# Row maxima in unequal column steps, and one VectorE instruction moved behind a transposition, in a routed-attention and feed-forward kernel

## The chip, the cores and the metric

The kernel runs on one core of one Trainium2 chip. The metric is the device time of one execution in microseconds (us); lower is better. A core has five engines that run at once, each through its own instructions in order: TensorE (PE in the profile; its weight loads are listed apart as PEld), VectorE (DVE), ScalarE (ACT), GpSimd (POOL) and SyncE (SP), which here only issues transfers. They wait for each other through semaphores. TensorE writes to PSUM, 128 partitions by 8 banks of 512 float32 values; everything else lives in SBUF.

## The reference

Two parts follow each other. The first is an attention in which a query sees only the keys that chose the same one of 16 centroids; the second is a feed-forward block on its output.

```python
batch, n_heads, seq, head_dim = (4, 8, 768, 64)      # n_clusters = 16
q_assign = np.argmax(np.einsum('bhsd,hcd->bhsc', q_n, c_n), axis=-1)
k_assign = np.argmax(np.einsum('bhsd,hcd->bhsc', k_n, c_n), axis=-1)
mask = q_assign[:, :, :, None] == k_assign[:, :, None, :]
scores = scale * np.matmul(q, k.transpose(0, 1, 3, 2))
scores = np.where(mask, scores, -1000000000.0)
scores = scores - np.max(scores, axis=-1, keepdims=True)
attn = np.exp(scores)
attn = attn / (np.sum(attn, axis=-1, keepdims=True) + 1e-09)
return np.matmul(attn, v).astype(np.float32)
...
h = x @ w_in                                          # x: 3072 x 512, w_in: 512 x 2048
sp = np.maximum(h, 0.0) + np.log1p(np.exp(-np.abs(h)))
g = h * erf(sp)
return (g @ w_out).astype(np.float32)
```

## The kernel before

The attention goes over 16 blocks `p`, each a batch and two heads; the two heads sit in partitions 0 to 63 and 64 to 127 and are worked on side by side. A block has 12 units: two halves of 384 queries, times six groups of 128 keys. A unit is a score matrix of 128 keys by 384 queries for both heads in a two-bank PSUM tile `sc`, of which there are two in turn. `products` (line 512) starts it with float32 products of keys and queries, `scores` (527) adds in bfloat16 the mask and the negative row maximum of each query (through `km` and `qm`), `curve` (541) takes the exponential on ScalarE into one of the eight tiles `pr`, `accumulate` (550) sums these on GpSimd, `attend` (562) multiplies them by the values on TensorE into `turned[half]`, and `divide` (575) normalizes a finished half.

The maximum of a query's row must be known before its scores. `maxima_step` (463) finds it half a block ahead: for a group `t` of 128 queries (`t` = 0 to 5) and one part of the keys, a bfloat16 pass over `qv` and `kv` and a pass over the masks `qm` and `km` fill the two-bank tile `wide`, one bank for each head, and a VectorE reduction over the part's columns writes the negative maximum into `nmx`. Each group of queries takes two such steps, over 384 keys each. There is one tile `wide`: a step can't start before the reduction of the step in front of it has read it. After three groups a small reduction writes `lowest`, and `turn` (494) transposes it into a row of `qm`.

`period(p, i)` (1345), six for each block, writes out the order of the work: two units and one group of queries, `t` = (i + 3) mod 6. On TensorE: the transposed `lowest` (i = 0, 3), the first maxima step, the products of two units, the first pass of the second step, the scores of the first unit, the second pass of the second step (on the array rows that the scores leave free), the scores of the second unit, `pick` matmuls that spread masks (`masks`, 437, in i = 0, 2, 5), the `similarities` (394) of block p + 2 with the centroids in i = 3, and the 32 matmuls of `attend` for the two units before. In i = 0 and 3 `divide` follows: its four sums go into `turned[1 - half]`, in i = 3 `turned[1]`, where the similarities of the same period lie until VectorE has transposed them.

`choose` (407) takes these similarities on VectorE: a transposition into `sims`, a maximum over each 16 (`mx`), a comparison (`hot`), and transpositions of that. In i = 3 `mx` is put into spare columns of the second unit's tile, `sc_of[u + 1]`, so this tile is free for its next unit, the second of i = 4, only when `hot` has read it.

Beside this, the weights of the second part are decoded from their transferred words, in pieces of 128 x 512 (28 of 32 pieces during the attention): `size`, `rest` and `sign` on ScalarE, `bounded` (322, a maximum with 2) and `shifted` (330, a shift left, on the result of `bounded`) on VectorE, `summed` (334) on GpSimd. A block decodes two pieces, one of which has `bounded` and `shifted` in i = 0, the other in i = 3, between the instructions of `choose`.

After the attention comes the feed-forward part, in a form with seven products of quarter matrices in place of eight; neither the diff nor the prediction goes into it.

All helpers record their instructions through one wrapper, so that nearly every row of the profile carries line 138; rows are told apart by the names of their tiles.

Of the kernel before, what the change touches and what calls it, by code (L numbers as in the profile page):

```python
# [14 lines left out]
ALU = mybir.AluOpType  # L15
ACT = mybir.ActivationFunctionType
AX = mybir.AxisListType
PSUM = bass.MemoryType.PSUM

P = 128  # L20
B, H, S, D = 4, 8, 768, 64
# [4 lines left out]
HW = S // 2  # L26
QW = HW // 2
TW = QW + 1
HJ = NJ // 2
HP = H // 2  # L30
NPAIR = B * HP
DM, DFF = H * D, 2048
NFT = DFF // P
# [113 lines left out]
def kernel(  # L147
# [53 lines left out]
    nbig = const.tile([P, 1], F32, name="nbig")  # L201
    ccT = const.tile([P, HP, 2 * C], F32, name="ccT")

# [22 lines left out]
    def heads(p):  # L226
        return p // HP, 2 * (p % HP)

    def load(p, nm, src, pl):
        if p >= NPAIR:  # L230
            return
        b, h0 = heads(p)
        if nm == "v":
            t = pl.tile([P, NJ, 2, D], F32, name="in_v")
            for e in range(2):
                queues[0].dma_start(out=t[:, :, e], in_=src[b, h0 + e].rearrange("(j p) d -> p j d", p=P))
        else:

            if pl is None:
                t = x_more.rearrange("p a k t -> p (a k t)")[:, (nm == "k") * S : (1 + (nm == "k")) * S]  # L240
                t = t.rearrange("p (n t) -> p n t", t=Q)
            else:
                t = pl.tile([P, NB, Q], F32, name="in_" + nm)
            for e in range(2):
                for g in range(D // Q):
                    queues[e if nm == "q" else e * g].dma_start(
                        out=t[e * D + g * Q : e * D + (g + 1) * Q],
                        in_=src[b, h0 + e, :, g * Q : (g + 1) * Q].rearrange("(n t) d -> t n d", t=Q),
                    )
        pairs.setdefault(p, {})[nm] = t  # L250
# [22 lines left out]
    for base, pattern, sign, op, fill in (  # L273
# [5 lines left out]
            out=first, in_=first, compare_op=op, fill=fill, base=base, pattern=pattern,  # L279
# [38 lines left out]
    def size_and_rest(n):  # L318
        size(n)
        rest(n)  # L320

    def bounded(n):
        w = w_steps[n][0]
        ve.tensor_scalar(out=w, in0=w, scalar1=2.0, scalar2=None, op0=ALU.max)
# [5 lines left out]
    def shifted(n):  # L330
        w = w_steps[n][0].bitcast(U32)
        ve.tensor_scalar(out=w, in0=w, scalar1=3, scalar2=None, op0=ALU.logical_shift_left)
# [8 lines left out]
    for e in range(2):  # L341
        for n in range(2):
            r = e * D + n * Q
# [37 lines left out]
    def transposes(p, which="qk"):  # L381

        if p >= NPAIR:
            return
# [9 lines left out]
    def similarities(p):  # L394

        if p >= NPAIR:
            return
        st = pairs[p]
        st["psim"] = turned[1][:, 0:HW]
        for g in range(4):  # L400
            te.matmul(
                st["psim"][2 * C * g : 2 * C * (g + 1)], lhsT=ccT[:, p % HP],
                rhs=st["qk"[g // 2] + "T"][:, (g % 2) * HW : (g % 2 + 1) * HW],
# [3 lines left out]
    def choose(p, spare=None, aside=False):  # L407

        if p >= NPAIR:
            return  # L410
# [22 lines left out]
    def vectors(p, nm):  # L433
        if p < NPAIR:
            ae.copy(out=pairs[p][nm + "v"], in_=pairs[p][nm + "T"])

    def masks(p, nm, half, bank, narrow=False, copied_by=ae):

        if p >= NPAIR:
            return lambda: None  # L440
# [22 lines left out]
    def maxima_step(p, i, sm=wide, behind=False):  # L463

        st = pairs[p]
        nmx = maxima[p % 2]
        t, half = divmod(i, 2)

        def passes(a, b, start, rows):
            for e in range(2):  # L470
                r = slice(e * D + rows.start, e * D + rows.stop)
                te.matmul(
                    sm[:, e, 0:HW], lhsT=st[a][r, t * P : (t + 1) * P],
                    rhs=st[b][r, half * HW : (half + 1) * HW], start=start, stop=not start,
                )

        passes("qv", "kv", True, slice(0, D))
        if behind:
            yield
        passes("qm", "km", False, slice(Q, D) if behind else slice(0, D))  # L480
        if behind:
            yield
        ve.tensor_reduce(
            out=nmx[:, :, t, half], in_=sm[:, :, 0:HW], axis=AX.X, op=ALU.max, negate=True
        )
        if i in (NJ - 1, 2 * NJ - 1):
            h = i // NJ
            ve.tensor_reduce(
                out=lowest[h][:, :, ::D].rearrange("p t e -> p e t"),
                in_=nmx[:, :, h * HJ : (h + 1) * HJ], axis=AX.X, op=ALU.min,  # L490
            )
            turns.append((p, h))
# [82 lines left out]
    def divide(u):  # L575
# [30 lines left out]
        )  # L606
        b, r = divmod(p, HP)
        for g in range(4):
# [717 lines left out]
    def run(work):  # L1326
        for _ in work:
            pass
# [16 lines left out]
    def period(p, i):  # L1345
        u = 2 * NJ * p + 2 * i
        n1, n2 = 2 * p - 1, 2 * p
        early = lambda n: 0 <= n < N_EARLY

        def mask(place):  # L1350
            which = (MASKS if p else FIRST_MASKS).get((i, place))
            if which:
                return masks(p + 1, *which, turned[0 if i in (0, 5) else 1], place > 1, ve if i == 0 else ae)
            return lambda: None

        if u > 0:
            for which in turns if i in (0, 3) else ():
                turn(*which)
                turns.remove(which)
            step_ahead(u)  # L1360
        mask(0)()
        next(part[0], None)
        if i == 5:
            next(routing[0], None)
        if i == 0 and p:
            run(routing[0])
        if u == 2:
            next(routing[0])
        products(u)
        products(u + 1)  # L1370
        mask(1)()
        second = step_ahead(u + 1, True) if u > 0 else iter(())
        next(second, None)
        rows = D if u == 0 or u + NJ >= len(units) else Q
        scores(u, rows)
        next(second, None)
        if i:
            next(second, None)
        next(part[0], None)
        scores(u + 1, rows)  # L1380
        later = mask(2)
        if i == 0:
            later()
            later = lambda: None
            next(second, None)
        if i == 3:
            similarities(p + 2)
            routing[0] = choose(p + 2, sc_of[u + 1][:, 0], True)
        curve(u)
        later()  # L1390
        curve(u + 1)
        if u == 0:
            step_ahead(1)
            similarities(1)
            routing[0] = choose(1, turned[0])
            next(routing[0])
            next(routing[0])
            vectors(1, "q")
            vectors(1, "k")
        if i == 0 and early(n1 - 1):  # L1400
            bounded(n1 - 1)
            shifted(n1 - 1)
            sign(n1 - 1)
        elif i == 1 and early(n1):
            size_and_rest(n1)
        elif i == 3 and early(n1):
            bounded(n1)
            sign(n1)
        elif i == 5 and early(n2):
            rest(n2)  # L1410
        for _ in range(min(len(forms), FORMS.get(p, {}).get(i, 0))):
            forms.pop(0)[0]()
        if i == 3:
            next(routing[0], None)
            if early(n1):
                shifted(n1)
            for _ in range(2):
                next(routing[0], None)
        elif i == 1:
            load(p + 1, "v", v, vp)  # L1420
            if p == 0:
                run(routing[0])
                transposes(2, "q")
        elif i == 2:
            transposes(p + 2, "k")
        elif i == 4:
            vectors(p + 2, "k")
            vectors(p + 2, "q")
        elif i == 5:
            transposes(p + 3, "q")  # L1430
        if u > 0:
            if i in POOL_FORMS.get(p, ()) and forms:
                forms.pop(0)[1]()
            if i == 1 and early(n1 - 1):
                summed(n1 - 1)
            elif i == 4 and early(n1):
                summed(n1)
            for w in (u - 2, u - 1):
                accumulate(w)
            for w in (u - 2, u - 1):  # L1440
                attend(w)
            if i % HJ == 0:
                part[0] = divide(u - 1)
                next(part[0])
        if i == 3 and early(n2):
            size(n2)
# [11 lines left out]
    st = pairs[0]  # L1458
    st["qT"], st["kT"] = rows[0]["q"], rows[0]["k"]
    ve.transpose(out=st["qT"], in_=st.pop("q").rearrange("p n t -> p (n t)"))  # L1460
    for e in range(2):
        ve.tensor_copy(
            out=ccT[e * D : (e + 1) * D, :, e * C : (e + 1) * C],
            in_=pct[e * D : (e + 1) * D].rearrange("d (r e c) -> d r e c", e=2, c=C)[:, :, e],
# [7 lines left out]
    for r in (0, D):  # L1472
        for half in range(2):
            for e in range(2):
                c = r + half * Q + e * C
                ve.tensor_copy(
                    out=pick[r : r + D, half, e * D : (e + 1) * D].rearrange("p (n c) -> p n c", n=2)[:, :, 1 : C + 1],
                    in_=first[r : r + D, c : c + C].unsqueeze(1).to_broadcast([D, 2, C]),
# [174 lines left out]
```

## Time and profile before

| | |
|---|---|
| time, median of 3 runs | 960.74 us (960.52 to 960.83) |
| the profiled execution: time, span | 960.8 us, 959.1 us |
| granted TensorE clock in it | 1.00 of full speed |
| the 192 maxima reductions on VectorE, 128 x 768 values each | 0.955 us each, 183 us in all |
| their matmuls, two passes, 2 x 378 | 63.9 and 62.6 us busy |
| attention, about 30 to 410 us: TensorE, VectorE, ScalarE, GpSimd busy | 380.0, 321.8, 288.0, 314.0 us |
| the rest, 410 to 959 us: the same | 545.3, 451.1, 238.7, 216.0 us |

The span is the time from the first to the last instruction in the trace; the device time is a little longer. In a timeline a row has the start, the time it took, the engine, the operation with the tile written and the tile read, the shape, and how many instructions were merged. An instruction is named by its tiles: `nmx<-wide` is a maxima reduction, `wide<-kv,qv` and `wide<-km,qm` are the two passes of a step, `sc<-...` with float32 (from `qT,kT`, or from `more_out`, where every third block keeps its `qT` and `kT`) are products, `sc<-qm,km` scores, `turned<-pr,in_v` is `attend`, `turned<-more_out,minus` the sums of `divide`. A VectorE `TENSOR_SCALAR` on `w_in` or `w_out` is `bounded` with type f32 and `shifted` with type uint32. Matmul rows overlap: their durations hold the passage through the array, so the distance of two starts tells what a matmul costs, not its duration.

### The profile page before, as it was taken

The numbers are of one execution on the slowest core, as the hardware profiler recorded it, in microseconds if no ns is written. First come the engines' busy times: TensorE is split into PE (matmuls) and PEld (weight loads), VectorE is DVE, ScalarE is ACT, GpSimd is POOL, SyncE is SP. The second block draws the span as 40 slices with busy tenths as digits, with TensorE's granted clock in tenths as the row PEclk, the third lists the DMA queues.
The fourth block names the chain that finished last, engine by engine and source line by source line (L and its number), as shares of the span: only waits on it lengthen the run. The fifth ranks groups of instructions, "written<-read, shape, count | busy, mean of one in ns | idle before, by whom it ended". The sixth has DMA issues, their size and how long they took to land.

```text
span 959.1 us, 22447 instructions
## 1 busy us (share of the span) xinstructions
PE 951.2 (99%) x8954; PEld 727.5 (76%) x8954; DVE 797.8 (83%) x1395; ACT 538.7 (56%) x815; POOL 538.3 (56%) x375
## 2 busy tenths in 40 slices
PE   8999999999999999999999999999999999999998
PEld 3555555555555555588888888998999899989987
DVE  8888888888888887787689889688868987897887
ACT  3777777777777777542524431654257236525541
POOL 1688888878888888897579910360054016203600
PEclk9999999999999999999999999999999999999999
DMA  9355444444454522041403444463444436343533
GB/s 217 68 112 112 111 111 111 112 112 111 90 119 83 133 54 57 21 151 55 177 1 154 157 161 145 130 199 110 154 133 165 116 126 210 110 149 121 159 112 110
DMA packets 172313, 116.06 MB, mean 121 GB/s; under 512 B 131376, under 2 KB 141104, under 8 KB 172208
## 3 DMA queue, kind: packets, MB, share of 16 engines
q1 hardware_dynamic: 169280, 113.41, 42.5%
q8 instruction: 71, 1.16, 0.5%
q10 hardware_dynamic: 2928, 1.21, 0.4%
q14 instruction: 34, 0.28, 0.1%
HBM read 90.21 MB, written 24.38 MB: 119 GB/s over the span
## 4 chain that ended last, share of the span: by engine, by line
PE 96%; DVE 2%; ACT 1%; issue 0%; DMA 0%; DVEq 0%; SPq 0%; ACTq 0%
PE bank L138 42%; PE turned L138 32%; PE sc L138 17%; PE wide L138 6%; DVE nmx L138 1%; ACT a_s L138 0%; ACT L138 0%; DVE g L138 0%; DMA in_q<-in_q_dram 0%; DVE kT L138 0%; DVE osb L138 0%; DVE g_more L138 0%; DVE sims L138 0%; DVE qT L138 0%; DVE turned L138 0%
## 5 line engine op out<-in xcount | busy, mean ns | idle before, releaser
L138 POOL TENSOR_TENSOR more_out<-more_out,pr 128x768 f32<-128x768 f32 x128 | 217.1, 1696 | 16.2 <-ACT pr L138 6.8
L138 DVE TENSOR_REDUCE nmx<-wide 128x2 f32<-128x768 f32 x189 | 180.5, 955 | 46.4 <-PE wide L138 45.9
L138 ACT ACTIVATE pr<-sc 128x768 f32<-128x768 f32 x192 | 148.7, 810 | 87.4 <-PE wide L138 68.7
L138 POOL TENSOR_TENSOR g<-g 128x512 f32<-128x512 f32 x36 | 47.1, 1310 | 217.2 <-DVE g L138 215.3
L138 PE MATMUL turned<-pr,in_v 128*32 128x193 f32 x3072 | 144.8, 330 | 0.0
L138 PEld LDWEIGHTS turned<-pr,in_v 128*32 128x32 f32 x3072 | 91.5, 109 | 50.7 <-issue 21.3
L138 PE MATMUL sc<-qT,kT 64*128 64x384 f32 x528 | 98.4, 486 | 0.0
L138 DVE TENSOR_TENSOR g<-g 128x512 f32<-128x512 f32 x114 | 79.0, 693 | 16.5 <-PE bank L138 12.9
L138 DVE TENSOR_TENSOR g<-a_s,g 128x512 f32<-128x512 f32 x80 | 73.4, 944 | 5.6 <-ACT a_s L138 5.6
L138 DVE TENSOR_TENSOR g<-bank,g 128x256 f32<-128x256 f32 (+1 forms) x129 | 63.8, 522 | 15.3 <-PE bank L138 8.1
L138 PE MATMUL bank<-w_out,g 128*128 128x256 f32 x328 | 75.7, 380 | 0.0
L138 ACT ACTIVATE a_s<-g 128x1024 f32<-128x1024 f32 (+1 forms) x36 | 41.0, 1149 | 56.1 <-POOL g L138 45.5
L138 PE MATMUL bank<-g_more,g 128*128 128x256 f32 x304 | 71.8, 379 | 0.0
L138 PE MATMUL bank<-x_own,w_in 128*128 128x128 f32 (+1 forms) x432 | 71.6, 308 | 0.0
L138 POOL TENSOR_TENSOR more_out<-pr,pr 128x768 f32<-128x768 f32 x32 | 58.9, 1840 | 20.3 <-ACT pr L138 20.3
L138 PEld LDWEIGHTS bank<-w_out,g 128*128 128x128 f32 x328 | 62.0, 190 | 9.6 <-issue 1.4
L138 PEld LDWEIGHTS <-qv 64*128 64x128 bf16 x384 | 27.0, 93 | 53.4 <-issue 37.4
L138 PEld LDWEIGHTS sc<-qT,kT 64*128 64x128 f32 x528 | 49.2, 187 | 22.0 <-ACT inv L138 3.1
L138 ACT ACT_TABLE_LOAD x40 | 51.3, 1283 | 24.3 <-DVE g L138 23.7
L138 PE MATMUL wide<-kv,qv 64*128 64x384 bf16 x378 | 63.9, 328 | 1.1 <-ACT km L138 0.6
L138 PEld LDWEIGHTS bank<-x_own,w_in 128*128 128x128 f32 x432 | 61.1, 191 | 4.0 <-issue 0.6
L138 PEld LDWEIGHTS bank<-g_more,g 128*128 128x128 f32 x304 | 57.8, 190 | 7.8
(242 smaller groups left out, 2065.5 us busy)
## 6 DMA issues: line engine op xcount, KB each, us to landing
g_more<-b_dram SPq DMA_DIRECT2D x48, 512.0 KB, 3.6
g_more<-w_dram SPq DMA_DIRECT2D x84, 256.0 KB, 2.8
x_own<-in_moe_w_in_dram SPq DMA_DIRECT2D x13, 512.0 KB, 5.1
in_v<-in_v_dram SPq DMA_DIRECT2D x32, 192.0 KB, 3.2
x_dram<-more_out SPq DMA_DIRECT2D x128, 48.0 KB, 1.7
x_own<-x_dram SPq DMA_DIRECT2D x6, 1024.0 KB, 5.5
in_k<-in_k_dram SPq DMA_DIRECT2D x59, 96.0 KB, 2.7
in_q<-in_q_dram SPq DMA_DIRECT2D x58, 96.0 KB, 4.9
```

Source lines behind the costliest of these rows:

```text
L138: ins = getattr(self.engine, name)(*args, **kw)
```

## The change

The columns of the two maxima steps of a group of queries become unequal: 256 and 512 keys for `t` = 0, 1, 3, 4, and 352 and 416 for `t` = 2 and 5. Both steps keep their place, their number of instructions and their sum of 768 keys. In period i = 3 `bounded` moves behind the next step of `choose`, which is the transposition into `sims`, and so comes directly in front of `shifted`; `sign`, on ScalarE, stays. On the other engines' queues and for the transfers the order is as it was.

```diff
+KEYS = (S - 512, S - 512, 352)
...
         t, half = divmod(i, 2)
 
+        n = KEYS[t % HJ]
+        keys = (slice(0, n), slice(n, S))[half]
+        n = keys.stop - keys.start
+
         def passes(a, b, start, rows):
             for e in range(2):
                 r = slice(e * D + rows.start, e * D + rows.stop)
                 te.matmul(
-                    sm[:, e, 0:HW], lhsT=st[a][r, t * P : (t + 1) * P],
-                    rhs=st[b][r, half * HW : (half + 1) * HW], start=start, stop=not start,
+                    sm[:, e, 0:n], lhsT=st[a][r, t * P : (t + 1) * P],
+                    rhs=st[b][r, keys], start=start, stop=not start,
                 )
...
         ve.tensor_reduce(
-            out=nmx[:, :, t, half], in_=sm[:, :, 0:HW], axis=AX.X, op=ALU.max, negate=True
+            out=nmx[:, :, t, half], in_=sm[:, :, 0:n], axis=AX.X, op=ALU.max, negate=True
         )
...
         elif i == 3 and early(n1):
-            bounded(n1)
             sign(n1)
...
         if i == 3:
             next(routing[0], None)
             if early(n1):
+                bounded(n1)
                 shifted(n1)
             for _ in range(2):
                 next(routing[0], None)
```

(S is 768, HW 384, HJ 3, P 128, D 64.)

## The prediction

> **What bounds the kernel now.** I read the page's shares first, then its chain of waits, then the timeline of one block of heads (head pair 11) engine by engine, and last the waits of the weight loads.
>
> ```profile
> PE 951.2 (99%) x8954; PEld 727.5 (76%) x8954; DVE 797.8 (83%) x1395; ACT 538.7 (56%) x815; POOL 538.3 (56%) x375
> ...
> PE 96%; DVE 2%; ACT 1%; issue 0%; DMA 0%; DVEq 0%; SPq 0%; ACTq 0%
> ```
>
> TensorE sets the end: 96% of the chain. Taken alone, this says that only streamed columns count and that VectorE, 83% busy, has room. The timeline says where it has none. First TensorE, period i=3 (starts and durations in us; below I use the trace's starts to the nanosecond):
>
> ```profile
> 299.80 0.34 PE L138 MATMUL wide<-kv,qv 64*128 64x384 bf16 x2
> 299.97 0.33 PE L138 MATMUL wide<-km,qm 64*128 64x384 bf16 x2
> 300.13 1.45 PE L138 MATMUL sc<-more_out 64*128 64x384 f32 x8
> 301.42 0.33 PE L138 MATMUL wide<-kv,qv 64*128 64x384 bf16 x2
> 301.68 0.33 PE L138 MATMUL sc<-qm,km 32*128 32x384 bf16 x2
> 301.69 0.34 PE L138 MATMUL wide<-km,qm 32*128 32x384 bf16 x2
> 301.85 0.32 PE L138 MATMUL sc<-qm,km 32*128 32x384 bf16 x2
> 302.11 0.52 PE L138 MATMUL turned<-qT,ccT 128*32 128x384 f32 x2
> ```
>
> The first maxima step of a period is the pair at 299.80 and 299.97, the second the pairs at 301.42 and 301.69. The two heads of a pair start 3 ns apart and run side by side, so a pass over 384 columns costs 0.16 to 0.17. The second pass of the second step (301.69) runs beside the scores of the first unit (301.68), and the scores of the second unit follow at 301.85. From one first step to the next there are 3.757 us in a period where TensorE waits for nothing (i=1 or 4 of the last blocks).
>
> Now VectorE from the second reduction of i=3 on, and the weight load that waits for it:
>
> ```profile
> 302.13 0.96 DVE L138 TENSOR_REDUCE nmx<-wide 128x2 f32<-128x768 f32 x1 [0.83 <-PE wide L138]
> ...
> 303.00 0.42 DVE L138 TENSOR_SCALAR w_out<-w_out 128x512 f32<-128x512 f32 x1
> 303.33 0.58 DVE L138 STREAM_TRANSPOSE sims<-turned 128x384 f32<-128x384 f32 x1
> 303.83 0.39 DVE L138 TENSOR_SCALAR w_out<-w_out 128x512 uint32<-128x512 uint32 x1
> 304.14 0.55 DVE L138 TENSOR_REDUCE sc<-sims 128x24 f32<-128x384 f32 x1
> 304.72 0.55 DVE L138 TENSOR_TENSOR hot<-sims,sc 128x384 bf16<-128x384 f32 x1
> 305.20 0.95 DVE L138 TENSOR_REDUCE nmx<-wide 128x2 f32<-128x768 f32 x1
> ```
>
> ```profile
> 305.39 0.33 PEld L138 LDWEIGHTS sc<-more_out 64*128 64x128 f32 x4 [0.34 <-ACT inv L138]
> ```
>
> VectorE runs without a gap from 302.13 to the reduction at 305.20. `hot` reads `mx`, which lies in the spare columns of the second unit's `sc` tile, so the next product into that tile waits for it. `hot` ends at 305.278; TensorE's queue passes a wait on VectorE's semaphore 0.040 later, the weight load starts 0.116 after `hot`, the product 0.226 after. In all 13 blocks (head pairs 1 to 13) these distances repeat within 3 ns. The profile names ACT as releaser, but ACT's `inv` had ended at 305.079. So this chain already meets TensorE to within 30 ns.
>
> The third place is i=0, where the second reduction stands behind the copy `km`:
>
> ```profile
> 314.80 0.62 DVE L138 TENSOR_SCALAR km<-turned,nbig 128x384 bf16<-128x384 f32 x1 [0.55 <-PE turned L138]
> 315.33 0.95 DVE L138 TENSOR_REDUCE nmx<-wide 128x2 f32<-128x768 f32 x1
> ...
> 316.20 0.92 DVE L138 TENSOR_SCALAR w_out<-w_out 128x512 f32<-128x512 f32 x2
> ...
> 316.36 0.34 PE L138 MATMUL wide<-kv,qv 64*128 64x384 bf16 x2
> ```
>
> That reduction ends at 316.283, and the first step of i=1 overwrites `wide` at 316.358: 0.075 apart, of which 0.054 is the handover (read where a pass does wait, i=4: 306.149 to 306.203). The slack is 0.02.
>
> **The change, columns first.** In i=0, 1, 3, 4 the first step has 256 columns and the second 512; in i=2, 5 they have 352 and 416. The 128-column matmuls of `lowest` start 0.055 apart, so 128 columns are worth 0.054. A first step saves two passes: 0.107 (0.027 in i=2, 5). In the second step the first pass costs 0.053 more (0.013). Its second pass costs nothing: started at 0.007 after the scores, it streams 0.22, while the scores of the second unit hold TensorE until 0.33. Where a `pick` matmul follows (i=0, 2, 5) it uses the same array rows as one half of that pass and waits for it, which gives back the gain: 0 in these. So TensorE gains 0.053 in each of i=1, 3, 4, if nobody makes it wait. The float32 weights behind the narrower pass were usable 0.09 to 0.11 after their load began (296.04, 305.39), the pass now lasts 0.107: I take 0, at worst 0.02 in each of 62 periods, 1 us in all.
>
> **Reductions.** 384 values take 0.550 (the row above at 304.14), 768 take 0.955: 1.055 ns a value. The short one becomes 0.69, the long one 1.225 (+0.265); in i=2, 5 they move by 0.067.
>
> **i=3 and i=4, times from the start of i=3 (299.798).** TensorE comes to the second step's second pass 0.053 earlier (0.107 won, 0.053 lost) and streams it 0.053 longer, so the reduction behind it still starts at 2.328; it ends at 3.553. Independent VectorE instructions start about 0.085 before the one in front ends, dependent ones 0.035 after. `sims` 3.468 to 4.044; the bound, now behind it, 3.968 to 4.386; the shift, which reads what the bound wrote and now stands right behind it, 4.421 (not 4.30) to 4.807; `mx` 4.724 to 5.277; `hot` 5.312 to 5.866. Before, `hot` ended at 5.480: 0.386 later, of which 0.265 is the reduction and 0.121 the move. What the move protects is real: the sums of `divide` (304.08, 4.286) need `turned[1]` free; with `sims` ending at 4.044 and 0.12 to 0.15 of handover they keep their new time 4.233. With the bound ahead they would be about 0.3 late.
>
> The product into the second unit could start at 5.547 but starts at 5.866 + 0.226 = 6.09. It runs 0.645 and 0.03 for its later half, so the second step comes at 6.77 at the latest; the short reduction (5.784 to 6.474) is not late. Scores at 7.08 (0.258 + 0.053 later), `attend` 0.427, the next first step 1.447 after that: i=5 starts at 8.954, before at 8.550. Plus 0.404 a block. Queued behind on VectorE are `den`, two products on `turned` and the second reduction of i=4; it ends at about 8.77, just in time.
>
> A rule of the Trainium skill speaks here, "VectorE: DVE Perf Modes", section "The DRAIN you can't avoid": chained operations cost the same with or without a semaphore between them, so the move by itself would be free. The trace disagrees: bound and shift back to back in i=0 start 0.490 apart (316.199, 316.689), while in i=3 the bound is followed after 0.332.
>
> **i=0.** `pick` ends as before (2.384 against 2.388 after the start of i=0), so `km` and the long reduction start as before; it ends 0.265 later, and i=1 starts at 4.33 instead of 4.089: plus 0.24. If the cover of 0.02 were larger, by so much less.
>
> **i=1.** Its short reduction ends at 1.38 after the start, the products at 1.519: TensorE no longer waits here. The mean of 14 such periods, 3.803, becomes 3.706: minus 0.10.
>
> **Others.** i=2 and i=5: 0, at worst 0.03 each if `lowest` (0.07 to 0.08 later) makes its transposition wait, 1 us in all. Blocks 0, 14 and 15, without bound or without similarities, together minus 0.15. The six reductions at the start, in the chain one after another, keep their sum and start 0.1 earlier. What follows the attention is bound by TensorE from the first matmul (it idles under 0.1 us between 396 and 950), so the delay reaches the end. ACT, POOL and the DMA queues keep their instructions and order.
>
> Sum: 13 x (0.404 + 0.24 - 0.10) = 7.1, less 0.2 is 6.9. The profiled execution took 960.8 (span 959.1 and 1.7 around it), 0.06 above the median: **967.7 us**, slower by 0.7%.
>
> **Rivals.**
> A, the move costs nothing: the shift follows the bound as closely as an independent instruction does, `hot` ends 0.121 earlier, 13 x 0.12 = 1.6 less: 966.1. For it: no instruction was added. Against: the pair in i=0. (It is what the skill's rule above says.)
> B, the named releaser is right and the product waits for ACT. Then the second step of i=4 waits for the short reduction alone, 6.474 + 0.054 = 6.53 instead of 6.77: 13 x 0.23 = 3.0 less: 964.7. For it: the label in brackets. Against: 40 ns behind `hot`, 13 times.
> C, faster: TensorE's columns decide alone, as the 96% suggest, and VectorE's lateness is covered everywhere. 16 blocks x 3 periods x 0.053, 13 waits of 0.05 in i=4 and 14 of 0.045 in i=1: 3.9 less, 956.9. It decides only if `hot` ends by 5.547 - 0.226 = 5.32 and the long reduction of i=0 by 4.03; worked out are 5.87 and 4.28.
> D, the second unit's scores wait until the 512-column pass has ended: 0.053 in four periods and 0.013 in two, 0.24 a block over 15.5 blocks: 3.7 more, 971.4. For it: matmuls start in order here. Against: those scores start at 301.85 on array rows of their own.
>
> **How the numbers follow.** Forecast 0.62, A 0.10, B 0.12, C 0.07, D 0.09. The range leaves out C and D: from B's 964.7 less 0.7 for the slopes, to the forecast plus the two worst cases of 1 us and 0.8 for the handovers, 964.0 to 970.5. About 0.2% is what a measurement here can tell from no change: faster 0.07 (C), within it 0.05 (B with a smaller stall in i=0), slower 0.88.
>
> **What would show it.** Right: reductions of 0.69 and 1.22; bound and shift 0.45 or more apart in i=3; `hot` 0.39 later from the start of i=3; a gap of half a microsecond in front of the second unit's product in i=4; i=0 at 4.33; i=5 at 8.95 after i=3. Wrong: reductions that do not scale, a product that starts while `hot` runs, or periods i=4 and i=0 near 3.7 and 4.09.

## The result, and the profile after

The changed kernel takes 970.23 us (median of 5 runs, 970.13 to 970.32), the kernel before 960.83 in the same comparison (960.52 to 961.2): a ratio of 1.0097, 95% interval 1.0086 to 1.0108. It is slower by 9.4 us, where 6.9 were forecast; the time lies inside the range. The profiled execution has a span of 968.5 us, before 959.1.

The page's shares and its chain of waits, after the change:

```profile
PE 954.0 (99%) x8954; PEld 721.8 (75%) x8954; DVE 800.7 (83%) x1395; ACT 538.7 (56%) x815; POOL 537.9 (56%) x375
...
PE 85%; DVE 11%; issue 2%; ACT 2%; DVEq 0%; ACTq 0%
...
L139 DVE TENSOR_REDUCE nmx<-wide 128x2 f32<-128x512 f32 (+1 forms) x189 | 179.1, 947 | 49.3 <-PE wide L139 47.6
L139 PE MATMUL sc<-qT,kT 64*128 64x384 f32 x528 | 100.7, 490 | 2.3 <-DVE hot L139 2.3
```

VectorE's busy time has hardly moved (800.7 for 797.8), and it is 83% busy as before; but its share of the chain went from 2% to 11%. The reductions still come to 0.947 each in the mean: their work is the same, only cut differently. The last row has a new releaser: products into `sc` wait for `hot`. TensorE's list of waits says how often (total, times, longest):

```profile
PE sc L139 <- DVE hot L139: 3.3, 13, 0.3
PE wide L139 <- DVE nmx L139: 0.9, 3, 0.4
```

13 times 0.25, once in each block that has all parts. Most of the 9.4 us is not in this list, since a row's duration holds the passage through the array and so covers a short gap behind it. So I measured each period on TensorE from one first maxima step to the next, in both traces (the median of the usual blocks, except where a mean is named):

| period | change in a usual block (1 to 13), us | sum over the attention, us |
|---|---|---|
| i=0 | +0.214 | +2.95 |
| i=1 | -0.094 (mean of 14) | -1.14 |
| i=2 | +0.103 | +1.44 |
| i=3 | -0.050 | -0.98 |
| i=4 | +0.407 | +5.42 |
| i=5 | 0 | 0 |
| all of the attention | | +7.69 |
| before its first i=3 | | +0.37 |
| behind the attention | | +1.37 |
| together | | +9.43 (span: 9.4) |

"Behind the attention", or the tail, is all that follows 403 us of the kernel before. In i=3 the sum is larger than 15 times -0.050, since in two blocks the kernel before took 0.14 and 0.16 longer there than in the rest.

Each place in turn. VectorE in i=3 and i=4 of block 11, to be laid beside the row of six that the prediction shows (the whole period there began at 299.80, here at 306.02):

```profile
308.30 1.23 DVE L139 TENSOR_REDUCE nmx<-wide 128x2 f32<-128x1024 f32 x1 [1.12 <-PE wide L139]
309.44 0.57 DVE L139 STREAM_TRANSPOSE sims<-turned 128x384 f32<-128x384 f32 x1
309.93 0.85 DVE L139 TENSOR_SCALAR w_out<-w_out 128x512 f32<-128x512 f32 x2
310.69 0.55 DVE L139 TENSOR_REDUCE sc<-sims 128x24 f32<-128x384 f32 x1
311.28 0.55 DVE L139 TENSOR_TENSOR hot<-sims,sc 128x384 bf16<-128x384 f32 x1
311.75 0.69 DVE L139 TENSOR_REDUCE nmx<-wide 128x2 f32<-128x512 f32 x1
```

The long reduction takes 1.23 (0.96 before), bound and shift now stand together (merged, x2, 0.85 for both), and `hot` ends at 311.83. TensorE in the same stretch:

```profile
310.92 0.81 PE L139 MATMUL sc<-more_out 64*128 64x384 f32 x4
311.99 0.92 PE L139 MATMUL sc<-more_out 64*128 64x384 f32 x4 [0.25 <-DVE hot L139]
312.70 0.41 PE L139 MATMUL wide<-kv,qv 64*128 64x512 bf16 x2
```

Before, the products of both units were one row of eight; now the second unit's four start 1.07 after the first's, with a gap in front of them, and the second maxima step follows them.

In i=0 it is the long reduction itself. VectorE and TensorE, block 12:

```profile
321.88 1.22 DVE L139 TENSOR_REDUCE nmx<-wide 128x2 f32<-128x1024 f32 x1
...
323.15 0.28 PE L139 MATMUL wide<-kv,qv 64*128 64x256 bf16 x2
```

It ends at 323.10, and the first step of i=1, which overwrites `wide`, starts 0.05 after it.

i=2 was forecast at nothing. One period further on:

```profile
325.55 1.22 DVE L139 TENSOR_REDUCE nmx<-wide 128x2 f32<-128x1024 f32 x1
326.68 0.55 DVE L139 SCALAR_TENSOR_TENSOR more_out<-den,turned 128x384 f32<-128x384 f32 x1
326.86 0.32 PE L139 MATMUL wide<-kv,qv 64*128 64x352 bf16 x2
327.02 0.31 PE L139 MATMUL wide<-km,qm 64*128 64x352 bf16 x2
327.28 0.32 PE L139 MATMUL turned<-hotT,pick 64*128 64x384 bf16 x1
327.29 1.60 PE L139 MATMUL sc<-qT,kT 64*128 64x384 f32 x8
```

The long reduction lets the first step of i=2 through without a wait. But behind it stands the last instruction of `divide`, `more_out<-den,turned`, which empties the bank of `turned` that `pick` fills next. It ends at 327.23, `pick` starts 0.05 later, and the products, which follow in order, start 0.43 after the first step of i=2 (0.34 before).

### The profile page after: what moved, and what is told of

Same layout as the page of the kernel before. It is cut to its first block, busy times and chain, and to the rows that moved or that the text cites. A ratio compares the mean times of both kernels' runs of the same rounds, so it can differ in the third digit from the quotient of the medians.

```text
span 968.5 us, 22434 instructions
## 1 busy us (share of the span) xinstructions
PE 954.0 (99%) x8954; PEld 721.8 (75%) x8954; DVE 800.7 (83%) x1395; ACT 538.7 (56%) x815; POOL 537.9 (56%) x375
## 4 chain that ended last, share of the span: by engine, by line
PE 85%; DVE 11%; issue 2%; ACT 2%; DVEq 0%; ACTq 0%
PE bank L139 39%; PE turned L139 25%; PE sc L139 16%; PE wide L139 5%; DVE nmx L139 4%; DVE g L139 1%; DVE km L139 1%; DVE sims L139 1%; DVE hot L139 1%; ACT a_s L139 1%; DVE sc L139 1%; DVE w_in L139 1%; DVE w_out L139 1%; ACT L139 1%; DVE g_more L139 0%
## 5 line engine op out<-in xcount | busy, mean ns | idle before, releaser
L139 DVE TENSOR_REDUCE nmx<-wide 128x2 f32<-128x512 f32 (+1 forms) x189 | 179.1, 947 | 49.3 <-PE wide L139 47.6
L139 PE MATMUL sc<-qT,kT 64*128 64x384 f32 x528 | 100.7, 490 | 2.3 <-DVE hot L139 2.3
L139 PE MATMUL wide<-kv,qv 64*128 64x256 bf16 (+1 forms) x378 | 63.9, 327 | 3.5 <-DVE nmx L139 0.9
L139 PEld LDWEIGHTS sc<-qT,kT 64*128 64x128 f32 x528 | 46.7, 187 | 25.1 <-ACT inv L139 7.8
L139 PE MATMUL wide<-km,qm 64*128 64x256 bf16 (+1 forms) x378 | 62.6, 326 | 0.0
```

The lines of the kernel that those rows point to most:

```text
L139: ins = getattr(self.engine, name)(*args, **kw)
```

## The experiments

Unless it is said otherwise the differences are against the kernel before, and periods are measured as in the table above. All ratios are against the kernel before, with their 95% intervals.

**The unequal steps without the move** (`e1_keys_only`).

```diff
         elif i == 3 and early(n1):
+            bounded(n1)
             sign(n1)
...
             if early(n1):
-                bounded(n1)
                 shifted(n1)
```

> The unequal steps alone; the bound stands in front of the transposition of the similarities again. Theory (a dependent neighbour costs about 0.12 on VectorE): in i=3 `hot` ends 0.12 earlier than in the changed kernel, so i=4 loses 0.12 less in 13 blocks, although the sums of `divide` now start some 0.2 late behind the transposition: 970.2 - 1.6 = 968.6 us, i=4 plus i=3 together 0.12 shorter than in the changed kernel. Rival A (the move costs nothing): the late sums remain and nothing is won, 970.2 or more.

Measured: 967.34 us (967.11 to 968.6), 1.0065 (1.005 to 1.008). VectorE in i=3 of one block:

```profile
207.52 1.23 DVE L139 TENSOR_REDUCE nmx<-wide 128x2 f32<-128x1024 f32 x1 [1.12 <-PE wide L139]
208.66 0.42 DVE L139 TENSOR_SCALAR w_in<-w_in 128x512 f32<-128x512 f32 x1
208.99 0.58 DVE L139 STREAM_TRANSPOSE sims<-turned 128x384 f32<-128x384 f32 x1
...
209.80 0.55 DVE L139 TENSOR_REDUCE sc<-sims 128x24 f32<-128x384 f32 x1
210.38 0.55 DVE L139 TENSOR_TENSOR hot<-sims,sc 128x384 bf16<-128x384 f32 x1
```

From the start of the long reduction to the end of `hot` are 3.41 us here and 3.53 in the changed kernel: without the move `hot` is 0.12 earlier. i=3 and i=4 together lose 0.230 a block where the changed kernel loses 0.357, 0.127 less (i=3 now +0.214, since `divide` waits for `turned[1]` when the bound stands ahead of `sims`, and i=4 +0.017). So the move costs 0.12 to 0.13 a block beside the long reduction, 13 times 1.65 in all. The time fell by 2.9 and not by 1.65, because the tail lost 0.03 here and 1.37 there, which has nothing to do with the block (below).

**The move without the unequal steps** (`e2_move_only`).

```diff
-KEYS = (S - 512, S - 512, 352)
+KEYS = (HW, HW, HW)
```

> Equal steps of 384, only the bound moved. Theory: `hot` and the short reduction behind it come 0.12 later, the second step of i=4 waits for that reduction: 13 x 0.12 = 1.6 us more than before, 962.4. Rival A: no difference, 960.8.

Measured: 965.17 us (964.56 to 965.32), 1.0038 (1.0024 to 1.0053). A move that adds no instruction costs 2.64 us in the attention (i=4: +0.233 a block; i=1 and i=3 give back 0.39 in all) and 1.74 behind it. Rival A, that it is free, falls; but my 0.12 was half of it. The last similarities on TensorE, and VectorE:

```profile
205.95 0.49 PE L139 MATMUL turned<-kT,ccT 128*32 128x384 f32 x2
205.61 0.96 DVE L139 TENSOR_REDUCE nmx<-wide 128x2 f32<-128x768 f32 x1 [0.83 <-PE wide L139]
206.58 0.58 DVE L139 STREAM_TRANSPOSE sims<-turned 128x384 f32<-128x384 f32 x1
207.09 0.85 DVE L139 TENSOR_SCALAR w_in<-w_in 128x512 f32<-128x512 f32 x2
```

`sims` starts after the reduction has ended (206.57), and not 0.085 before, as an instruction does that waits for nothing: the last similarities reach `turned` only at 206.44 (205.95 + 0.49), and it waits for them: in the trace VectorE's queue passes the wait on TensorE's semaphore at 206.53, and `sims` starts 0.05 later. Before, the bound filled this time. So the move costs 0.12 for the dependent pair and 0.11 for a wait that the bound had covered; behind the long reduction of the changed kernel this wait is gone, and there 0.12 is right.

**`mx` in a tile of its own** (`e3_mx_apart`). The changed kernel, with `mx` in SBUF in place of the spare columns of `sc`, so that no product has to wait for `hot`.

```diff
-        mx = (wide[:, 0] if spare is None else spare)[:, 512 - n :]
+        if aside:
+            mx = routep.tile([P, n], F32, name="mx")
+        else:
+            mx = (wide[:, 0] if spare is None else spare)[:, 512 - n :]
```

> The changed kernel, with `mx` in a tile of its own instead of the spare columns of the second unit's `sc`, so that no product waits for `hot`. Theory (the product waits for `hot`): the product of i=4 starts at 0.88 after the start of i=4 instead of 1.29, and the wait moves to the second step, which follows the first reduction at 1.80 instead of 2.01: 0.21 to 0.24 a block, 13 blocks, 3 us less, 967.2. Rival B (the releaser was ACT): the gap stays and so does the time, 970.2.

Measured: 980.31 us (979.96 to 981.42), 1.0199 (1.0184 to 1.0214), ten slower than the changed kernel. The claim about the wait holds and the price was missed altogether:

```profile
216.25 1.46 PE L139 MATMUL sc<-qT,kT 64*128 64x384 f32 x8
216.50 1.29 POOL L139 TENSOR_TENSOR w_in<-w_in,x_own 128x512 int32<-128x512 int32 x1 [2.05 <-ACT x_own L139]
216.60 1.60 DVE L139 TENSOR_TENSOR hot<-sims,mx 128x384 bf16<-128x384 f32 x1
218.13 0.68 DVE L139 TENSOR_REDUCE nmx<-wide 128x2 f32<-128x512 f32 x1
218.86 0.39 PE L139 MATMUL wide<-kv,qv 64*128 64x512 bf16 x2 [1.15 <-DVE nmx L139]
```

The eight products of both units are one row again, while `hot` still runs. The new tile removes only the wait on `hot`; `inv`, the releaser that the profile of before names, is where it was. Rival B falls with this. But `hot` itself takes 1.60, where it took 0.55, while an addition on GpSimd runs from 216.50 to 217.79; the reduction behind it is late, and the second maxima step waits 1.15. In every block, as the groups of the changed kernel and of this one say:

```profile
L139 DVE TENSOR_TENSOR hot<-sims,sc 128x384 bf16<-128x384 f32 x14 | 7.8, 554 | 0.5
```

```profile
L139 DVE TENSOR_TENSOR hot<-sims,mx 128x384 bf16<-128x384 f32 x14 | 22.2, 1585 | 0.5
```

The Trainium skill, "SBUF — State Buffer", section "Who interferes with whom", says that a VectorE instruction with two SBUF inputs contends with a GpSimd instruction that reads SBUF; the trace agrees, 0.554 to 1.585. In all 14 blocks `hot` ends 0.42 after GpSimd's instruction does, also in block 0, where that one had begun 0.79 before `hot` (in the others 0.11) and `hot` took only 1.45: its end follows GpSimd's. Where `mx` lay in `sc` before, it was in PSUM, and this did not happen. In no block is GpSimd idle there, so what `mx` in SBUF would cost without it is not shown.

**Equal steps in i=0 alone** (`e4_even_i0`). The changed kernel with 384 and 384 keys in the step of i=0 (`t` = 3).

```diff
-KEYS = (S - 512, S - 512, 352)
+KEYS = (256, 256, 352, HW, 256, 352)
...
-        n = KEYS[t % HJ]
+        n = KEYS[t]
```

> The changed kernel with equal steps in i=0 alone (t = 3). Theory: i=0 falls back from 4.30 to 4.09, but in i=1 `den` waits for `inv`, which follows the sums of `divide` and not the start of i=1, so the long reduction of i=1 starts at 2.67 instead of 2.40 after the start of i=1, ends at 3.89 and holds up i=2: i=1 becomes about 3.94 instead of 3.71. Nearly all is given back: 970.2 plus or minus 0.5. Rival (the terms of the prediction add): 14 x 0.21 = 3.0 us less, 967.2.

Measured: 970.66 us (970.5 to 970.87), 1.0097 (1.0082 to 1.0112): as slow as the whole change. The 0.214 of i=0 are gone, but i=1 has turned from -0.094 to +0.13 in the mean, and i=2 from +0.103 to +0.14: 0.27 for the three periods, where the changed kernel pays 0.223. TensorE's list of waits says where the stall went:

```profile
PE sc L139 <- DVE hot L139: 3.3, 13, 0.3
...
PE wide L139 <- DVE nmx L139: 2.3, 14, 0.3
```

Now the first step of i=2 waits for the long reduction of i=1. In the changed kernel the stall in i=0 makes TensorE so late that VectorE has caught up by then: the long reduction of i=1 starts 2.41 after its period there, and 2.67 here, as in the kernel before.

**The unequal step in i=1 alone** (`e5_only_i1`). The kernel before, with 256 and 512 keys for `t` = 4 only.

```diff
-KEYS = (S - 512, S - 512, 352)
+KEYS = (HW, HW, HW, HW, 256, HW)
...
-        n = KEYS[t % HJ]
+        n = KEYS[t]
```

> The kernel before with 256 and 512 in i=1 alone (t = 4), nothing else. Theory: `den` waits for `inv` as before, so the long reduction of i=1 starts at 2.67 as before, ends 0.27 later and holds up the first step of i=2 by about 0.15; behind it on VectorE stands `more_out<-den,turned`, which frees the bank that the `pick` matmul of i=2 writes, so the products of i=2 come another 0.10 to 0.14 late. 14 blocks x 0.25 to 0.29 = 3.5 to 4.0 us: about 964.7, plus up to 1.8 if VectorE and GpSimd meet badly in the second part. Rival (the 0.10 in i=2 has another cause): i=2 stays at 4.09, 963.0.

Measured: 964.47 us (964.09 to 965.56), 1.0038 (1.0023 to 1.0052); i=1 +0.10 to +0.15, i=2 +0.12. The one period that gained in the changed kernel loses when it stands alone:

```profile
321.46 1.22 DVE L139 TENSOR_REDUCE nmx<-wide 128x2 f32<-128x1024 f32 x1
322.59 0.55 DVE L139 SCALAR_TENSOR_TENSOR more_out<-den,turned 128x384 f32<-128x384 f32 x1
```

```profile
322.73 0.34 PE L139 MATMUL wide<-kv,qv 64*128 64x384 bf16 x2 [0.16 <-DVE nmx L139]
...
323.19 0.32 PE L139 MATMUL turned<-hotT,pick 64*128 64x384 bf16 x1
```

The reduction ends at 322.68 and TensorE waits 0.16 for it; `more_out<-den,turned` ends at 323.14 and `pick` starts 0.05 after it. Both stalls behind one reduction are in these four rows.

**A plain delay at the end of the attention** (`e6_late_6`, `e7_late_12`). The kernel before with 6 or 12 matmuls that nobody needs, in the last block, to see what a delay by itself does to the rest.

```diff
+        if (p, i) == (NPAIR - 1, 4):
+            warm(6, wide[:, 0], zeros)
```

> The kernel before with 6 more matmuls of 384 columns into the unused tile `wide` in the last block, after the last maxima step: TensorE alone is put off by about 1.0 us against the engines beside it, and nothing else is changed. Theory (the 1.37 us that the changed kernel lost behind the attention come from VectorE and GpSimd meeting in another phase): the end moves by 1.0 plus something between 0 and 1.8, and the places 447 and 473 us show it. Rival (it comes from the edit itself): the end moves by 1.0, 961.9.

> The same with 12 such matmuls, 2.0 us. Theory: 2.0 plus a loss behind the attention that differs from that with 6, between 0 and 1.8. Rival: 2.0 in all, 962.9.

Measured: 962.55 us (962.29 to 963.21), 1.0018 (1.0008 to 1.0028), and 963.13 (962.77 to 963.31), 1.0021 (1.0011 to 1.0032). The matmuls delay TensorE by 1.10 and 2.08 up to 403 us; from there to the end the profiled executions lose another 0.72 and 0.30. With six matmuls this speaks against the rival (961.9); with twelve the time is within 0.3 of the rival's 962.9 and decides nothing by itself. Where such a loss comes from is seen in how VectorE and GpSimd meet behind the attention. First VectorE and GpSimd before, then after:

```profile
421.33 0.42 DVE L138 TENSOR_SCALAR w_out<-w_out 128x512 f32<-128x512 f32 x1
421.36 1.54 POOL L138 TENSOR_TENSOR a_s<-w_in 128x512 f32<-128x512 f32 x1
422.86 0.42 DVE L138 TENSOR_SCALAR w_out<-w_out 128x512 uint32<-128x512 uint32 x1
```

```profile
429.42 1.28 POOL L139 TENSOR_TENSOR a_s<-w_in 128x512 f32<-128x512 f32 x1
429.44 1.53 DVE L139 TENSOR_SCALAR w_out<-w_out 128x512 f32<-128x512 f32 x1
432.08 1.29 POOL L139 TENSOR_TENSOR w_out<-w_out,g_more 128x512 int32<-128x512 int32 x1
432.08 1.57 DVE L139 TENSOR_SCALAR w_out<-w_out 128x512 uint32<-128x512 uint32 x1
...
456.79 1.10 PE L139 MATMUL turned<-x_own,w_in 128*128 128x256 f32 x4 [0.43 <-DVE g L139]
```

Before, the bound on VectorE started 0.02 ahead of GpSimd's instruction (0.023 by the trace's nanoseconds) and took 0.42, and GpSimd's took 1.54; after, GpSimd started 0.03 ahead (0.028), took 1.28, and the bound took 1.53. The shift meets the same a little later, so VectorE falls 2.3 us further behind, and TensorE, which has a reserve there, still waits 0.43 for `g`. At 447 us (in the time of the kernel before) the changed kernel has lost 0.89 in this way, at 473 another 0.50.

The same two instructions in all ten profiles (us; `e8_small` is the next experiment). How far VectorE falls behind is how much later than before its shift ends, less the delay that TensorE has there:

| run | the bound starts, against GpSimd's instruction | bound and shift take | VectorE falls behind TensorE by | lost behind the attention |
|---|---|---|---|---|
| before | 0.02 ahead | 0.42, 0.42 | 0 | 0 |
| e1 | 0.02 ahead | 0.42, 0.42 | 0.01 | 0.03 |
| e5 | 0.02 ahead | 0.42, 0.42 | 0.02 | 0.21 |
| after | 0.03 behind | 1.53, 1.57 | 2.33 | 1.37 |
| e2 | 0.11 behind | 1.45, 1.57 | 2.30 | 1.74 |
| e3 | 0.01 behind | 1.56, 1.56 | 2.31 | 1.39 |
| e4 | 0.13 behind | 1.45, 1.58 | 2.33 | 1.39 |
| e8 | 0.09 behind | 1.47, 1.58 | 2.33 | 1.71 |
| e6 | 0.32 behind | 1.24, 1.57 | 1.39 | 0.72 |
| e7 | 0.34 behind | 1.23, 1.57 | 1.09 | 0.30 |

Where the bound comes first next to nothing is lost; where it comes second, VectorE falls behind and the loss follows how far. In e6 and e7 the matmuls have put TensorE itself off, so that VectorE is less far behind it. (e2 and e8 lose about 0.35 more at 694 us and e5 0.17, from a cause that stays open.) How late TensorE leaves the attention doesn't decide the order: 0.97, 2.64, 8.05, 8.31 and 19.14 us have the bound second, 3.09 and 6.59 have it first. What does decide between instructions a few hundredths apart is not shown, and it may not need an edit at all: beside e8 the kernel before ran 13 times, eight times in 960.45 to 961.47 us and five times in 962.15 to 963.31. None of these five was traced, so whether they had this loss is open. The five times of the changed kernel lie within 0.19 us, so that its 1.37 probably stands in all of them.

**A small inequality** (`e8_small`). 352 and 416 keys for every group, the bound in its old place.

```diff
-KEYS = (S - 512, S - 512, 352)
+KEYS = (352, 352, 352)
```

> All six groups of queries in steps of 352 and 416, the bound in its old place: a quarter of the shift. Theory (each place has a slack of its own, and TensorE has at most 0.013 to win in a period): the long reductions end 0.067 later; i=0 has 0.02 of cover and loses 0.04, i=1 and i=2 lose up to 0.07 between them, i=3 and i=4 together stay within 0.05 of the kernel before: 0.05 to 0.12 a block, 961.5 to 962.7 us, plus what the second part adds by phase. Rival C in small (columns decide): 0.04 a block less, 960.2.

Measured: 962.09 us (961.63 to 963.48), 1.0009 (0.9999 to 1.0018). In the attention it loses 1.00 us, 0.063 a block (i=0 +0.03, i=2 +0.075, i=3 +0.05, against gains in i=1 and i=4); as a whole (its profiled execution is the slowest of its ten) it can't be told from the kernel before. No size of step that was run beats it.

## Why the prediction was right, and where it was not

**i=3 and i=4: right.** Forecast 0.404 a block, measured 0.357. The steps: long reduction 1.227 (1.225); bound to shift 0.419 (0.453: the bound itself took 0.384 and not 0.418, but the shift, 0.035 behind its end as forecast, took 0.427 and not 0.386, so the pair costs what I took within 0.01); end of `hot`, from the start of i=3, 5.820 (5.866); second unit's product 5.968 (6.09); scores 0.427 ahead of `attend`, as before; i=5 at 8.905 (8.954). The 0.047 too much come from one place: the long reduction started at 2.279 and not at 2.328, 0.052 behind the end of its pass, where the trace of before had 0.103 in i=3; why is not shown. Another misreading is hidden in it: I took 0.226 from `hot` to the product. That was the distance in a trace in which TensorE, too, was only just arriving; where it really waits, in this trace, the distance is 0.148. That this did no harm is luck: behind the wait the product's second pass follows the first after 0.397 and not after 0.322, which gives the 0.078 back.

**i=0: right.** +0.214 for a forecast 0.24; the long reduction ends 0.053 before the step that it lets through. e4 adds what the prediction didn't say: undoing this term brings nothing back.

**i=1: right in size, for the changed kernel only.** -0.094 for -0.10. e5 shows that the gain stands on the stall in i=0 in front of it.

**i=2: wrong.** Forecast 0, at worst 0.03; measured +0.103, 1.44 us in all. The step that failed reads "i=2 and i=5: 0, at worst 0.03 each if `lowest` (0.07 to 0.08 later) makes its transposition wait": I looked only at what follows on the maxima, and not at what else stands in VectorE's queue behind the long reduction of i=1. That is the last instruction of `divide`, and what waits for it is the bank for `pick`. The rows of block 12 and e5 show it.

**Blocks 0, 14 and 15: wrong by little.** I took together -0.15; measured are +0.37, of which i=2 of block 14 is 0.11. Block 14 lost 0.19 in i=4, block 15 0.18 in i=1, while smaller gains in block 0 and in 15 made up for part. There the product `den` waits on VectorE for ScalarE's `inv`, so a shorter first reduction does not bring the long second one, which is queued behind `den`, any nearer.

**Behind the attention: wrong.** "The delay reaches the end" unchanged, I wrote, since TensorE idles under 0.1 us there. It was 1.37 more. That idle time told only that VectorE was in time in this one execution. The table of the ten profiles shows what was overlooked: in the kernel before, the bound is only 0.02 ahead of GpSimd's instruction, and where it comes second without TensorE being put off, as in five of the profiles, 1.37 or more is lost. I could have bounded this (0 to 1.7, as the runs now show) but not forecast it.

**The start: not settled.** Forecast -0.1, measured +0.37. In the experiments' profiles the same stretch is between 0.36 shorter (e5) and 0.55 longer (e3) than before. It has not been tried by itself.

The sum: forecast 13 x (0.404 + 0.24 - 0.10) = 7.1; measured 13 x (0.357 + 0.214 - 0.094) = 6.2. Without i=2 (1.44), the tail (1.37) and the start (0.37) the forecast would have been a little too high; with them it was 2.5 too low. That the time lies inside the range, 0.3 below its upper end, is therefore partly luck: the 2.8 us that the range had above the forecast were for late weights, a late `lowest` and slower handovers, and i=5 at 0 and i=3 at -0.050 show none of these; what filled it were the three terms that had no allowance.

**The rivals.** A, the move is free: e1 and e2 against it. B, ACT releases the product: e3 against it, and the profile after names `hot` itself. C, TensorE's columns alone decide: every experiment with unequal steps against it; even e8, with the least shift, loses in the attention. D, the long pass holds up the second unit's scores: `attend` still comes 0.427 after the scores, so no.

## What to carry to other kernels

Where one engine is busy all the time and another fills its gaps exactly, cutting a piece of work unevenly makes the long half late by all it gained, and gives the short half's time back only where somebody was waiting for it; look at everything that stands in the queue behind the long half, not just at who reads its result. Undoing one of several stalls in a row shows little, since the next one takes its place: price them together. And where two engines reach a place within a few hundredths of a microsecond of each other, a change far in front of it can turn their order, as it did here; look for such places behind the change, and allow for them in the range.

## What the runs showed of the hardware

A VectorE instruction with two inputs in SBUF, the second only 128 x 24 values that are repeated, took 1.585 in place of 0.554 beside GpSimd's instructions, and ended 0.42 after them each time. A VectorE bound took 0.42 when it started 0.02 ahead of GpSimd's instruction and 1.53 when it started 0.03 behind it; in all seven profiles in which it started behind, it ended 0.28 after GpSimd's. Reductions from PSUM followed the number of values: 0.69 for 512 (0.655 in i=0 and 3), 0.96 for 768, 1.22 for 1024. A VectorE instruction that reads the result of the one in front started 0.035 after that one's end, an independent one 0.085 before it. And a 512-column pass on 32 array rows beside two passes of 384 on others cost TensorE nothing that could be read: the scores of the second unit started 0.173 after those of the first, as before.
